# Identity products in TensorE's gaps, another order of the first loads, and a re-planned order, in a fused attention and mixture-of-attention-experts kernel

## The chip, the core and the metric

The program runs on one core of one Trainium2 chip. A core has four computing engines that run side by side, each with its own instruction stream in a fixed order: TensorE (PE, matrix products; PEld are its weight loads), VectorE (DVE), ScalarE (ACT, functions such as tanh and exp) and GpSimd (POOL). SyncE (SP) only issues transfers (DMAs) between the chip's memory and the on-chip memory; ACT and POOL can issue some too. Engines wait for each other by semaphores. The metric is the device time of one execution in microseconds (us); lower is better.

## What is computed

Two stages follow each other. The first is attention over 8 batches of 12 heads, 448 positions, head size 64, with soft-capped scores; its output, 8 x 448 x 768, is the input of the second: four causal attention experts per batch, two of them chosen for each position by a gate.

```python
def _attn_ref(q, k, v, cap):
    scores = cap * np.tanh(scale * (q @ k.T) / cap)
    attn = softmax(scores)                  # over keys
    return attn @ v

def _moe_ref(x, w_gate, wq, wk, wv, wo):
    topk = argpartition(-(x @ w_gate), 2)[..., :2]; w = softmax of the two logits
    for e in range(4):
        q, k, v = x @ wq[e], x @ wk[e], x @ wv[e]
        a = causal_softmax(q @ k.T / 8)
        out += (w of e where chosen, else 0) * (a @ v @ wo[e])
```

## The kernel before

**Tiling.** Two heads of a batch form a pair; there are 48 pairs, six to a batch. For each pair:

- loads of k, q and v into f32 staging tiles (`kst`, `vst`, four each, two pairs in one; `qf`). k and v come in three parts: 384 rows, and the last 64 rows of the even and of the odd head (`kt0`, `kt1`, `vt0`, `vt1`).
- casts to f16 (`cast`, L399): by POOL, but by DVE for some k of early pairs (`CV`) and for q and k of the first pairs; pair 0's k by ACT.
- transposes of q and k so that the head size lies on the partitions: by products with an identity on PE and a copy out of PSUM by DVE (`a_tr` L441, `a_trev` L469), and from pair 9 on for k, from pair 34 on for q too, by a transposing DMA on SP (`a_trd` L475).
- scores on PE (`sc`, L541), in three groups with one tanh each on ACT (`y`, L547): two blocks of 448 columns (tanh over 128 x 896), or three (128 x 1344). The two products of a block pair have 64 rows each and use different halves of the array.
- one exp on ACT over all seven blocks (`pbuf`, L560).
- attention times values on PE (`pv`, L572 and L577) in four parts (two PSUM tiles, two halves each), normalisation by DVE (`xk`, L589), a transpose (`xtp`, L599) and a copy to `xT`, the second stage's input.

When six pairs of a batch are done, the second stage of that batch is interleaved with the pairs that follow: values and gate (`vps`, L679), projections (`qps`, `kps`, L801), masks, scores and exp (`pS`, L827), values, output projection (`wops`, L908) and stores. Its weights `wvg`, `wq`, `wk` and `wo` are loaded by DMAs that POOL issues (L1302) between its casts.

**What sets the order.** A planner in the kernel file (class `Sched`) writes out every engine's instructions while the program is built. Each unit of work has an engine, an assumed duration, units it needs, and a due time; among the units that can start first the one with the smallest due time is taken. Transfers are given an assumed landing. Nothing is timed on the chip: an engine's instructions simply stand in the planned order and wait for their semaphores. The planner's parameters are constants at the head of the file: `EA` (earliest planned load of some pairs), `AHEAD` (how far ahead of a pair its loads are planned), `WD` (planned times of the weight DMAs), `CV`, `LATE`, and `DUES` (offsets on the due times by kind of work). The list `FIRST` fixes order and queue of the first loads by hand; SP issues most of them, ACT three:

```python
FIRST = [
    ("k", 0, 1, "SP"), ("kt0", 0, 2, "SP"), ("k", 1, 1, "SP"), ("q", 1, 1, "SP"),
    ("v", 0, 1, "SP"), ("vt0", 0, 2, "SP"), ("kt0", 2, 2, "SP"), ("kt1", 2, 2, "SP"),
    ("k", 2, 1, "SP"), ("q", 2, 1, "SP"), ("v", 1, 1, "SP"), ("k", 3, 1, "SP"),
    ("q", 3, 1, "SP"), ("vt0", 2, 2, "SP"), ("vt1", 2, 2, "SP"), ("v", 2, 2, "SP"),
    ("q", 0, 1, "ACT"), ("kt1", 0, 2, "ACT"), ("vt1", 0, 2, "ACT"),
]
```

PE begins with seven products of a zero tile (`dummy`, L1333). For pair 0, ACT casts 384 columns of k and copies their transposes, DVE does q; scores begin when both are copied.

Of the kernel before, what the change touches and what calls it, by code (L numbers as in the profile page):

```python
# [16 lines left out]
NAUX = 3  # L17
# [3 lines left out]
LATE = 7  # L21
TD = 15.0
EA = {4: 0.0, 6: 0.0, 8: 8.0, 10: 20.0, 12: 40.0, 14: 50.0}
# [3 lines left out]
CV = 8  # L27
# [3 lines left out]
AHEAD = 34.0  # L31
WD = (22.0, 26.0, 38.0, 50.0)
DUES = {
    'B0': 1, 'B2': 6, 'B3': 19, 'B4': -16, 'g5': -1001, 'gw5': 16, 'gw6': -1000, 'laff': 1,
    'lf': 8, 'lg': -1000, 'llg': -1000, 'lotev': 1000, 'lpv': 16, 'lpvev': -1000, 'lqk': 1000,
    'lv': -1, 'lwo': 1016, 'mk5': 4, 'mk6': -8, 'oa6': 1016, 'pv46': -6, 'pvB6': -4, 'pvev46':
    -2, 'pvevA': 6, 'q6': 3, 'qm6': -1000, 'v5': -2000, 'wo6': -2, 'xt45': 1, 'xtA': -5,
    'xtev45': -2, 'xtev46': 12, 'xtev47': 2, 'xtevA': 1000
# [3 lines left out]
class Sched:  # L42
# [58 lines left out]
    def arm(self, u):  # L101
# [6 lines left out]
        for d in u["deps"]:  # L108
            t, e = self.done[d]
            x = 0.0  # L110
            if e == "POOL" and u["eng"] != "POOL":
                x = max(PS, u["slack"] if u["eng"] == "PE" else 0.0)
            elif u["eng"] == "PE" and e != "PE":
                x = u["slack"]
            r = max(r, t + x)
# [3 lines left out]
    HALF = ("tr", "trq", "trk", "trt", "xt", "mk", "oT", "lot", "keep")  # L119
# [13 lines left out]
    def start(self, u, e=None):  # L133
        s = max(self.free[e or u["eng"]], u["r"])
        if u["eng"] == "DVE" and u["key"][0] in self.PORT:
            s = max(s, self.free["POOL"])
# [4 lines left out]
    def emit(self, u, e):  # L141
# [10 lines left out]
        if e == "PE":  # L152
            dur += 0.1 if self.mode == 64 else 0.0
            self.mode = 128
# [3 lines left out]
        if u["land"]:  # L158
            self.dma = max(self.dma, s + 2.0) + u["land"] / 2.15e5
            t = self.dma + 0.1 + u["lag"]  # L160
        if u["give"] is not None:
            self.bank[self.held.pop(u["give"])] = t
# [3 lines left out]
        self.finish(u["key"], t, e)  # L166

# [73 lines left out]
def kernel(  # L241
# [113 lines left out]
    def nbytes(n, which):  # L355
        t = {"q": 224 * 0.055, "k": 256 * 0.045, "v": 256 * 0.045}.get(which, 64 * 0.03)
        return n * t / 16 * 2.15e5
# [3 lines left out]
        ("k", 0, 1, "SP"), ("kt0", 0, 2, "SP"), ("k", 1, 1, "SP"), ("q", 1, 1, "SP"),  # L361
        ("v", 0, 1, "SP"), ("vt0", 0, 2, "SP"), ("kt0", 2, 2, "SP"), ("kt1", 2, 2, "SP"),
        ("k", 2, 1, "SP"), ("q", 2, 1, "SP"), ("v", 1, 1, "SP"), ("k", 3, 1, "SP"),
        ("q", 3, 1, "SP"), ("vt0", 2, 2, "SP"), ("vt1", 2, 2, "SP"), ("v", 2, 2, "SP"),
        ("q", 0, 1, "ACT"), ("kt1", 0, 2, "ACT"), ("vt1", 0, 2, "ACT"),
    ]

    def add_load(p, n, w, due, e, deps, after=0.0):
        add(
            ("ld", w, p), e, 0.62, deps, due, load_part, p, n, w,  # L370
            nc.scalar if e == "ACT" else nc.sync, land=nbytes(n, w), lag=(DF + 1.5 * (p < 4) if p < 10 else LG if p > 15 else 0.0) if p > 1 else 0.0,
# [6 lines left out]
    for x, (w, p, n, e) in enumerate(FIRST):  # L378
        d = [last.get(e)] + ([("zst", w[0], p // 2)] if len(w) > 1 else [])
        d += [("table",)] if e == "ACT" and x > 17 else []  # L380
# [20 lines left out]
    def cast(w, p, eng):  # L401
        src = staged.pop((w, p))
        cp = eng.copy if eng is nc.scalar else eng.tensor_copy
        if w == "q":
            c16["q", p] = hd.tile([QP, QC, 2, Dh], f16, name=f"q16_{p}", tag="q16", bufs=NC)
            cp(c16["q", p], src.rearrange("p h (c d) -> p c h d", c=QC))  # L406
        elif w == "k":
            c16["k", p] = hd.tile([128, KC + 1, 2, Dh], f16, name=f"k16_{p}", tag="k16", bufs=NC)
            n = KC if p == 0 else KC + 1
            cp(c16["k", p][:, 0:n], src.rearrange("p h c d -> p c h d")[:, 0:n])  # L410
            if p == 0:
                staged["kt", p] = src[:, :, KC, :]
        elif w == "kt":
            cp(c16["k", p][:, KC], src)
# [3 lines left out]
    def add_cast(p):  # L418
        for w in CASTS:
# [11 lines left out]
            if p == 0 and w == "k":  # L431
                eng, ne, c = nc.scalar, "ACT", 0.42
                add(("cast", "kt", p), "DVE", 0.2, [("cast", "k", p)] + deps[1:], due, cast, "kt",
                    p, nc.vector)
# [8 lines left out]
    def a_tr(p, what="qk"):  # L443
# [10 lines left out]
        for c in {"qk": (0, 1, 2, 3), "k": (0, 1, 2), "t": (3,)}.get(what, ()):  # L454
# [14 lines left out]
    def a_trev(p, what):  # L469
        t = qk_tile(p)  # L470
        lo, hi = {"qk": (0, S + 512), "q": (0, S), "k": (S, S + KM), "t": (S + KM, S + 512)}[what]
# [11 lines left out]
    def add_tr(p):  # L483
# [4 lines left out]
        if p == 0:  # L488
            for w, d in (("k", "k"), ("q", "q"), ("t", "kt")):
                add(("tr" + w, p), "PE", 0.14 * len(w), [("cast", d, p), ("ident",)], due, a_tr, p,  # L490
                    w, take=("tr" + w, p), slack=0.0)
                add(("trev" + w, p), "ACT" if w == "k" else "DVE", 0.4, [("tr" + w, p)], -50.0,
                    a_trev, p, w, give=("tr" + w, p))
            add(("trev", p), "-", 0.0, [("trevk", p), ("trevq", p)], -50.0, lambda: None)
            add(("tr", p), "-", 0.0, [("trt", p)], -50.0, lambda: None)
            return
        if p >= FIRST_D:
            for w in "qk" if p >= FIRST_Q else "k":
                add(("trd" + w, p), "SP", 1.2, [("cast", w, p)] + deps[2:], due - TD, a_trd, p, w,
                    land=1.05 * 2.15e5)  # L500
# [797 lines left out]
    def add_weight(key, pairs, due):  # L1298
        due += 2.0
        for i, (dst, src) in enumerate(pairs):  # L1300
            def go(dst=dst, src=src):
                nc.gpsimd.dma_start(dst, src)  # L1302
            add((*key, i), "POOL", 0.85, [], due + i, go, after=due - 2.0 + i, land=1.3 * 2.15e5)
# [26 lines left out]
    def c_dummy():  # L1330
        ps = ps_score[0].tile([128, CAPS[0], 512], f32, name="dummy", tag="sc0")
        for _ in range(7):
            nc.tensor.matmul(ps[:, 0, :], warm[:, 0:128], warm, start=True, stop=True)  # L1333

# [73 lines left out]
    add(("table",), "ACT", 1.6, [("warm",), ("ld", "kt1", 0, "issued")], -300.0, c_table)  # L1408
# [45 lines left out]

    def pairs_of(i, later=0):
# [5 lines left out]
        if i >= NK or ("trev", i) not in sch.done:  # L1461
            return None
        return i, sch.done["trev", i][0] + 0.05

    def next_fill():
# [14 lines left out]
        if ("trev", i) not in sch.done:  # L1480
            return None
        r = max(r, sch.done["trev", i][0] + 0.05)
        one = dict(r=r, dur=0.4, armed=armed, special=True, go=lambda s: go_t([i], s))
        if nf < 1 or not info[i]["rem"]:
# [39 lines left out]
    def go_x(x, s, dur):  # L1524
        b, a = x
        sc = tile_of(state["nf"] % 2)
# [12 lines left out]
    def go_t(which, s):  # L1539
        todo = []  # L1540
# [98 lines left out]
```

## Time and profile before

| what | value |
|---|---|
| median of 3 runs | 319.39 us (319.07 to 320.24) |
| the profiled execution, its own time | 319.31 us |
| its span, first to last instruction | 317.0 us |
| mean granted TensorE clock | 0.953 of full |
| ACT: tanh (L547), 144 instructions | 144.0 us |
| ACT: exp (L560), 47 instructions | 136.6 us |
| first tanh starts at | 6.58 us |
| HBM read and written over the span | 149 GB/s |

The profile was taken from one execution by the hardware profiler. "Busy" is the time in which an engine had an instruction of its own; issuing DMAs and waiting for semaphores do not count. The granted clock is the share of the full TensorE clock that the chip's throttle let through. A timeline row gives start, duration, engine and line, operation, output from input with shapes, and in brackets the idle time of the engine just before it and what ended it.

The first transfers of the trace, with issue and landing in us:

| transfer | queue | issued | landed |
|---|---|---|---|
| k of pair 0 | SP | 0.80 | 4.57 |
| q of pair 0 | ACT | 0.81 | 4.26 |
| kt0, pairs 0 and 1 | SP | 1.50 | 5.60 |
| kt1, pairs 0 and 1 | ACT | 1.51 | 5.11 |
| k of pair 1 | SP | 2.30 | 6.92 |
| vt1, pairs 0 and 1 | ACT | 2.33 | 6.19 |
| q of pair 1 | SP | 3.17 | 7.90 |
| v of pair 0 | SP | 3.75 | 8.25 |
| k, q of pair 2 | SP | 6.37, 7.00 | 9.20, 9.84 |
| v of pair 1 | SP | 7.92 | 12.17 |
| k, q of pair 3 | SP | 8.33, 8.84 | 12.73, 13.30 |

### The profile page before, as it was taken

The page shows a single profiled execution, that of the slowest core. Times are in us where ns is not written, and L with a number is a line of the kernel's source. Part 1 is how long each engine was busy: PE and PEld are TensorE (multiplying, and loading weights), DVE is VectorE, ACT ScalarE, POOL GpSimd, SP SyncE. Part 2 cuts the span into 40 slices and gives each one's busy share as a digit, 9 for nine tenths or more (in the row PEclk, how much of TensorE's full clock was granted, in tenths as well). Part 3 has the DMA queues.
Part 4 walks back from the last instruction along what each step waited for, and adds up shares of the span by engine and source line. Part 5 has one row for each costly group of instructions (what it writes and reads, how often), then busy time and mean ns, then how long its engine had stood idle before and what let it go on. Part 6 is the DMA issues. An engine that isn't in the chain of part 4 may idle for free.

```text
span 317.0 us, 8054 instructions
## 1 busy us (share of the span) xinstructions
PE 273.1 (86%) x3073; PEld 175.3 (55%) x3073; DVE 203.2 (64%) x660; ACT 290.1 (92%) x229; POOL 177.3 (56%) x342
## 2 busy tenths in 40 slices
PE   6678669988899989998899989998899989989891
PEld 2355435665556655566656655765456755656650
DVE  2177442757667586667876675688577677664972
ACT  4889997999999999999999999999999999995631
POOL 6579690599707774498512993994419834421500
PEclk9577987999999999999999999999999999999978
DMA  6999999475979349961899484955988751020027
GB/s 158 270 280 216 232 200 185 109 152 127 276 189 223 81 113 216 302 151 36 232 260 226 82 205 83 290 174 118 278 250 198 165 104 63 0 77 2 0 97 254
DMA packets 93190, 52.87 MB, mean 167 GB/s; under 512 B 53792, under 2 KB 89760, under 8 KB 93152
## 3 DMA queue, kind: packets, MB, share of 16 engines
q1 hardware_dynamic: 81888, 50.19, 64.9%
q0 software_dynamic: 10512, 1.58, 7.0%
q10 hardware_dynamic: 752, 0.59, 0.8%
q8 instruction: 24, 0.39, 0.5%
q14 instruction: 14, 0.11, 0.2%
HBM read 36.19 MB, written 11.01 MB: 149 GB/s over the span
## 4 chain that ended last, share of the span: by engine, by line
ACT 60%; PE 24%; issue 5%; DVE 5%; POOL 2%; DMA 1%; POOLq 0%; ACTq 0%; DVEq 0%
ACT pbuf L560 28%; ACT y L547 26%; PE sc L541 5%; ACT pS L827 4%; PE pv L577 3%; PE sc L820 2%; PE vps L679 2%; PE qps L801 2%; PE pv L572 2%; DMA kst<-in_k_dram 1%; PE kps L801 1%; PE end L1050 1%; POOL ee L741 1%; PE wops L908 1%; PE xtp L599 1%
## 5 line engine op out<-in xcount | busy, mean ns | idle before, releaser
L547 ACT ACTIVATE y<-sc 128x896 f16<-128x896 f32 x144 | 144.0, 1122 | 5.2 <-PE sc L541 5.2
L560 ACT ACTIVATE pbuf<-y 128x3136 f16<-128x3136 f16 x47 | 136.6, 2906 | 0.0
L541 PE MATMUL sc<-qk 64*128 64x448 f16 (+1 forms) x336 | 63.1, 371 | 10.9 <-ACT y L547 6.8
L577 PE MATMUL pv<-v,pbuf 128*128 128x65 f16 x1140 | 60.7, 196 | 0.0
L577 PEld LDWEIGHTS <-pbuf 128*128 128x128 f16 x1152 | 53.5, 99 | 5.3 <-issue 2.5
L572 PE MATMUL pv<-v,pbuf 128*128 128x130 f16 x190 | 43.1, 227 | 13.0 <-ACT pbuf L560 10.1
L541 PEld LDWEIGHTS <-qk 64*128 64x128 f16 (+1 forms) x336 | 20.1, 94 | 44.3 <-issue 37.3
L406 POOL CAST q<-qf 112x512 f16<-112x512 f32 x46 | 28.2, 615 | 26.0 <-DMA qf<-in_q_dram 25.7
L589 DVE TENSOR_TENSOR xk<-pv,rc 128x256 f16<-128x256 f32 x95 | 40.3, 424 | 3.3
L727 POOL COPY mb<-mk 128x1024 f16<-128x1024 f16 x14 | 14.2, 1039 | 48.5 <-DVE mk L722 48.5
L572 PEld LDWEIGHTS <-pbuf 128*128 128x128 f16 x192 | 18.9, 98 | 25.6 <-ACT pbuf L560 15.4
L588 DVE RECIPROCAL rc<-pv 128x4 f32<-128x4 f32 x95 | 16.8, 177 | 23.5 <-PE pv L577 23.0
L416 POOL CAST v<-vst 128x512 f16<-128x512 f32 x48 | 28.3, 616 | 6.4 <-DMA vst<-in_v_dram 6.2
L835 POOL TENSOR_TENSOR pS<-pS,keep 128x128 f16<-128x128 f16 (+1 forms) x56 | 21.0, 395 | 15.9 <-ACT pS L827 14.3
L629 DVE COPY xT<-xtp 128x448 f16<-128x448 f16 x48 | 18.4, 386 | 17.4 <-PE xtp L599 17.4
L923 DVE COPY ob<-wops 128x384 f32<-128x384 f32 (+1 forms) x48 | 25.5, 554 | 5.9 <-PE wops L908 5.2
L679 PE MATMUL vps<-wvg,xT 128*128 128x260 f16 x168 | 29.0, 283 | 0.0
L410 POOL CAST k<-kst 128x512 f16<-128x512 f32 x42 | 25.7, 614 | 0.5 <-DMA kst<-in_k_dram 0.3
L908 PE MATMUL wops<-wo,oT 128*128 128x384 f16 x112 | 24.9, 326 | 0.5 <-DVE o L873 0.2
L741 POOL TENSOR_TENSOR ee<-euler,lg 128x16 f32<-128x16 f32 x7 | 20.4, 2913 | 8.6 <-DVE lg L686 8.6
L801 PE MATMUL qps<-xT,wq 128*128 128x448 f16 x84 | 23.3, 366 | 0.0
L801 PE MATMUL kps<-xT,wk 128*128 128x448 f16 x84 | 22.2, 352 | 0.9 <-DVE ob L923 0.4
(172 smaller groups left out, 429.6 us busy)
## 6 DMA issues: line engine op xcount, KB each, us to landing
qf<-in_q_dram SPq DMA_DIRECT2D x22, 448.0 KB, 5.5
vst<-in_v_dram SPq DMA_DIRECT2D x23, 384.0 KB, 5.0
kst<-in_k_dram SPq DMA_DIRECT2D x22, 384.0 KB, 4.7
out_dram<-ob SPq DMA_DIRECT2D x18, 384.0 KB, 3.0
kst<-in_k_dram SPq DMA_DIRECT2D x47, 32.0 KB, 4.9
vst<-in_v_dram SPq DMA_DIRECT2D x47, 32.0 KB, 4.4
out_dram<-ob SPq DMA_DIRECT2D x6, 192.0 KB, 2.9
out_dram<-vst SPq DMA_DIRECT2D x3, 384.0 KB, 2.3
```

The lines of the kernel that those rows point to most:

```text
L406: cp(c16["q", p], src.rearrange("p h (c d) -> p c h d", c=QC))
L410: cp(c16["k", p][:, 0:n], src.rearrange("p h c d -> p c h d")[:, 0:n])
L416: cp(v16[p % NV][:, :, :, 0:Dh], src)
L541: nc.tensor.matmul(o, kk[r, 128 * c : 128 * (c + 1)], qs, start=True, stop=True)
L547: nc.scalar.activation(ytile[i][:, first : first + nb, :], sc[:, 0:nb, 0:S], AF.Tanh, scale=isc / capf)
L560: nc.scalar.activation(ptile[i], ytile.pop(i), AF.Exp, scale=capf)
L572: nc.tensor.matmul(pv[:, n, :, :], ptile[i][:, idx[0, KC], w : w + 128], v16[i % NV][:, :, KC, :], start=(n == 0), stop=False, skip_group_ ...
L577: nc.tensor.matmul(pv[:, n, g, :], ptile[i][:, idx[g, c], w : w + 128], v16[i % NV][:, g, c, :], start=False, stop=(c == KC - 1), skip_gro ...
L589: nc.vector.tensor_tensor(xk, pv[:, :, :, 0:Dh], rc.broadcast_to((128, 2, 2, Dh)), ALU.mult)
L679: nc.tensor.matmul(ps, xT[b][:, j, w : w + 128], wvg[:, j, :], start=(j == 0), stop=(j == NDC - 1),)
L801: nc.tensor.matmul(s[which, r], w2[r][:, j, :], xT[b][:, j, :], start=(j == 0), stop=(j == NDC - 1),)
L908: nc.tensor.matmul(ps, s["oT"][:, r, w : w + 128], wo2[r][:, f * (D // 2) : (f + 1) * (D // 2)], start=(r == 0), stop=(r == 1),)
```

## The change

Four things change.

1. Products of the identity with itself, 128 columns each, are put where the planner sees PE idle before 60 us of planned time (`keep_warm`, `warmer`). Their output is never read. The program has 76 of them, in groups.
2. The first loads change order and queue: q of pair 1 goes to ACT's queue, `vt1` to SP's. Pair 0's k is cast and transposed in three pieces (128 columns by ACT, 256 by DVE, the tail by DVE), and scores may begin when the first piece is there. Pair 1's q and k are transposed and copied separately.
3. The planner's model of transfers (bytes by kind, latency, lag) and of some port rules has other numbers.
4. `DUES`, `EA`, `AHEAD`, `WD`, `CV` and `LATE` have other values, so that the planned order differs over most of the program.

```diff
-LATE = 7
+LATE = 9
-EA = {4: 0.0, 6: 0.0, 8: 8.0, 10: 20.0, 12: 40.0, 14: 50.0}
+EA = {4: 0.0, 6: 0.0, 8: 20.0, 10: 12.0, 12: 52.0, 14: 30.0}
-CV = 8
+CV = 6
-AHEAD = 34.0
-WD = (22.0, 26.0, 38.0, 50.0)
+WARM = 60.0
+AHEAD = 37.0
+WD = (18.0, 26.0, 40.0, 50.0)
 DUES = {
...
@@ def emit(self, u, e):
         if e == "PE":
+            self.keep_warm(s)
...
-            self.dma = max(self.dma, s + 2.0) + u["land"] / 2.15e5
+            self.dma = max(self.dma, s + (2.6 if s < 3.0 else 2.2)) + u["land"] / 2.15e5
...
+    def keep_warm(self, s):
+        f = self.free["PE"]
+        n = int((s - f - 0.1) / 0.115)
+        if not 4.0 < f < WARM or s > 1.0e6 or n < 3:
+            return
+        i = min(range(NAUX), key=lambda i: self.bank[i])
+        if self.bank[i] > f:
+            return
+        self.nw = getattr(self, "nw", 0) + n
+        self.warm(self.pool.tile([128, 512], f32, name=f"warm_{self.nw}", tag=f"aux{i}"), n)
...
-        ("k", 0, 1, "SP"), ("kt0", 0, 2, "SP"), ("k", 1, 1, "SP"), ("q", 1, 1, "SP"),
-        ("v", 0, 1, "SP"), ("vt0", 0, 2, "SP"), ("kt0", 2, 2, "SP"), ("kt1", 2, 2, "SP"),
+        ("k", 0, 1, "SP"), ("kt0", 0, 2, "SP"), ("k", 1, 1, "SP"), ("v", 0, 1, "SP"),
+        ("vt0", 0, 2, "SP"), ("vt1", 0, 2, "SP"), ("kt0", 2, 2, "SP"), ("kt1", 2, 2, "SP"),
...
-        ("q", 0, 1, "ACT"), ("kt1", 0, 2, "ACT"), ("vt1", 0, 2, "ACT"),
+        ("q", 0, 1, "ACT"), ("kt1", 0, 2, "ACT"), ("q", 1, 1, "ACT"),
...
+            lo, hi = {"k": (0, 1), "kb": (1, KC), "kt": (KC, KC + 1)}[w] if p == 0 else (0, KC + 1)
+            cp(c16["k", p][:, lo:hi], src.rearrange("p h c d -> p c h d")[:, lo:hi])
...
-                eng, ne, c = nc.scalar, "ACT", 0.42
-                add(("cast", "kt", p), "DVE", 0.2, [("cast", "k", p)] + deps[1:], due, cast, "kt",
-                    p, nc.vector)
+                eng, ne, c = nc.scalar, "ACT", 0.25
+                add(("cast", "kt", p), "DVE", 0.2, deps[1:], due, cast, "kt", p, nc.vector)
+                add(("cast", "kb", p), "DVE", 0.33, deps[0:1], due, cast, "kb", p, nc.vector)
...
+    def warmer(ps, n):
+        for _ in range(n):
+            nc.tensor.matmul(ps[:, 0:128], ident, ident, start=True, stop=True)
+
+    sch.warm = warmer
```

PE's order at the first pairs, as the two programs have it (number of products; `tr` are transposes of a pair, `sc` score groups, three to a pair, `pv a` and `pv b` the two tiles of attention times values):

```
before: dummy 7 | q0 4, k0 3, tail 1 | sc0 2, sc1 2, sc2 3 | tr1 8 | sc3 2, sc4+sc5 5
        | pv0 a, pv0 b | tr2 8 | pv0 a, pv0 b | sc6 2, sc7 2 | tr3 8 | sc8 3 ...
after:  dummy 7 | q0 4, k0 1, k0 2 | sc0 2, sc1 2 | tail 1 | 3 products | q1 4 | sc2 3 | k1 4
        | 5 products | sc3 2 | 9 products | sc4+sc5 5 | tr2 8 | 9 products | tr3 8
        | pv0 a, pv0 b, pv0 a, pv0 b | sc6 2 | x0 4 | sc7 2, sc8 3 ...
```

Further on, groups of 8, 16, 13 and 13 products stand before the pv of pairs 1, 3, 4 and 5. On DVE, the cast of q1 stands before the copy of pair 0's tail transpose. On POOL, the casts come in the order v0, k2, q2, v1, k3, q3 (before: v0, v1, k2, q2, k3, q3), and the four DMAs of `wk` stand after the casts of k10, k11, v9 and v10 (before: ahead of all four but v9). On SP, the loads of pairs 14 and 15 stand before the transposing DMAs of pairs 9 to 11, and the loads of pairs 12 and 13 after the transposing DMAs of pairs 14 and 15. ACT's sequence is unchanged but for the two first copies and the place of two exps of the second stage (`pS` of batch 0). On every engine the last instructions, the second stage of the last two batches and the last pairs' scores, stand as before.

## The prediction

> **What bounds the kernel now.** I read the page first: which engine is nearly always busy, and in which of the 40 slices something is off.
>
> ```profile
> PE 273.1 (86%) x3073; PEld 175.3 (55%) x3073; DVE 203.2 (64%) x660; ACT 290.1 (92%) x229; POOL 177.3 (56%) x342
> PEclk9577987999999999999999999999999999999978
> ```
>
> ScalarE (ACT) works 290.1 of 317.0 us; 26.9 us are idle. The clock row shows TensorE throttled in the first seven slices, some 55 us. The table of stretches then says where ACT idles: 8.7 us before 60, none from 60 to 280 (a row of it below), 18.1 after 280.
>
> ```profile
> 80.00:120.00 40.00, 35.96 (x432) 23.60 (x430) 27.50 (x90) 40.00 (x31) 22.86 (x41) 1.00 0.70 174
> ```
>
> The order of the last pair and the last batch is the same in both programs, so the 18.1 us at the end stay. ACT's operations are the same too, but for two copies cut from 384 to 128 columns. The change can therefore earn only what ACT waits before 60 us, and lose by new waits after it. ACT's waits, then its timeline at those waits (start, duration, in brackets the idle time before it):
>
> ```profile
> ACT y L547 <- PE sc L541: 5.2, 6, 1.8
> ...
> 8.63 1.29 ACT L547 ACTIVATE y<-sc 128x1344 f16<-128x1344 f32 x1 [0.32 <-PE sc L541]
> 10.74 0.92 ACT L547 ACTIVATE y<-sc 128x896 f16<-128x896 f32 x1 [0.82 <-PE sc L541]
> 17.75 0.92 ACT L547 ACTIVATE y<-sc 128x896 f16<-128x896 f32 x1 [1.40 <-PE sc L541]
> 29.14 0.92 ACT L547 ACTIVATE y<-sc 128x896 f16<-128x896 f32 x1 [0.29 <-PE sc L541]
> 53.03 0.92 ACT L547 ACTIVATE y<-sc 128x896 f16<-128x896 f32 x1 [1.79 <-PE sc L541]
> ```
>
> All five are tanh waiting for scores: 4.6 us, and 0.56 before the first tanh at 6.58. So 5.2 us is the whole stake of the first 60.
>
> **The clock.** It changes at multiples of 3.41 us from 3.94. I cut the span there (PE busy, PEld, DVE, ACT, POOL, granted clock, DMA, GB/s):
>
> ```profile
> 3.94:7.36 3.42, 1.74 (x14) 0.69 (x13) 1.46 (x5) 1.77 (x3) 1.91 (x20) 1.00 0.83 217
> 17.60:21.01 3.41, 1.86 (x19) 0.93 (x15) 2.89 (x21) 3.26 (x2) 2.12 (x4) 1.00 1.12 294
> 31.25:34.66 3.41, 2.01 (x43) 1.59 (x40) 1.75 (x6) 3.41 (x4) 2.82 (x6) 1.00 1.66 226
> 41.49:44.90 3.41, 1.36 (x24) 0.89 (x24) 0.13 (x1) 3.41 (x3) 3.41 (x8) 1.00 1.26 252
> 44.90:48.32 3.42, 2.97 (x21) 1.32 (x20) 1.47 (x5) 3.42 (x3) 1.97 (x4) 0.50 1.66 206
> ```
>
> After the first, second and fourth the clock is 0.50 in the next window; after the third it stays at 1.00. Busy time (1.86 against 2.01) hardly separates them; streamed columns do. Summed over the matmuls of each window (the two 64-row products of a score pair run side by side and count once) they are 0.23, 0.29 and 0.25 of what full clock could stream where the clock fell (8192 columns), and 0.38 (34.66:38.07) and 0.44 where it stayed. So the bound lies between 0.29 and 0.38, 2400 to 3100 columns a window.
>
> The Trainium skill, "TensorE: Matmul & The Clock Gate", section "Why this matters for your kernels", allows PE-idle gaps up to some 3 us. By it the products would be useless, since PE's longest idle stretch in the cooled window 41.49 to 44.90 is 2.05 us; the row shows a fall all the same. By the rule the sum below would lose its 1.79; the measurement decides.
>
> **Part 1, the products (L1366).** 76 in the program, 128 columns each, all before the first batch's projections: groups of 3, 5, 9, 9, 8, 16, 13, 13. A transpose of that size steps at 0.11 us at half clock (0.63 for four at 8.76) and about 0.055 at full (0.39 for four at 18.01, 0.22 of it the first one's latency).
> - 41.49 window: 13 products are 1664 columns, 0.25 + 0.20 = 0.45: above the bound. Then the block of scores, values and q projections in front of the sc at 52.57 runs at full clock: 5.9 us (46.64 to 52.57) become about 3.5 (5.09 of them halve), and the stall of **1.79** goes, with 0.6 to spare. If only half of the 13 fall into the window, 0.35 is between the bounds and the stall may stay.
> - 17.60 window: 8 products add 1024 columns, 0.29 + 0.12 = 0.41. The pair's four pv parts at 24 to 28 us then take 0.25 instead of 0.41 each, and **0.29** at 29.14 goes.
> - First window: only 3 products fall in it; 0.23 + 0.05 + the 448 columns of pair 1's q if they come in time = 0.28 to 0.33. I take it that the clock falls at 7.36 as before.
> They hide in PE's waits, except where they run at half clock right before ready work: nine cost 0.96 us (counted below).
>
> **Part 2, loads, casts and transposes of pairs 0 to 3.**
> - First tanh. ACT's cast of k falls from 0.51 to about 0.30 us (384 to 128 columns; 0.83 ns a column from the 0.92 and 1.29 of tanh), its copy from 0.48 to 0.27. Then the q copy on DVE, which ends at 5.18 + 0.39 = 5.57 now, decides; scores follow 0.16 later as now, tanh 0.40 after them: 6.13 instead of 6.58.
> - Pair 1. q1 moves from third on SP to ACT's queue, issued at 2.33 instead of 3.17, beside k1 on SP. Now q1 lands 4.7 us after issue (7.90), k1 4.6 (6.92). No row has two large first loads side by side: q1 lands at 6.6 at best (224 KB behind kt1's 5.11, at 150 of the first window's 217 GB/s) and 7.9 at worst (as now). I take 7.2. New waits: DVE's cast of q1 stands ahead of the tail copy that sc needs, and on PE the transposes of q1 stand ahead of pair 0's third scores; both now wait for that landing. From it, at half clock: cast 0.43, transposes 0.37, three scores 0.75, four k transposes 0.43 and latency 0.20, copy 0.41, gaps 0.14, scores 0.59 = 3.3. Pair 1's tanh starts at 10.5 (9.9 to 11.2) instead of 10.74; third scores come at 9.1, a wait of about 1.1, inside this number.
> - The skill's "DMA: Bandwidth & Descriptors", section "Queues, rings and completion order", says that each DMA engine takes turns between the queues with work; by that both k1 and q1 would end near 7.4, my estimate, and the tanh at 10.7. No run here shows it.
> - Pair 2, the 1.40. Now POOL casts v1 first, which lands late, and k2, q2, k3, q3 queue behind it:
>
> ```profile
> 12.22 0.62 POOL L416 CAST v<-vst 128x512 f16<-128x512 f32 x1 [3.04 <-DMA vst<-in_v_dram]
> ...
> 14.45 0.61 POOL L406 CAST q<-qf 112x512 f16<-112x512 f32 x1
> ```
>
>  After the change k2 and q2 (landed 9.84) go ahead of v1, so pair 2's transposes leave PE's way. But pair 3's now stand before pv of pair 0: q3 lands 13.30 as now (the same bytes are ahead of it), its cast is third behind v1 and k3 and ends at 13.33 + 0.61 = 13.94. PE at half clock: nine products, 1.04 of scores, 0.9 of pair 2, nine products end about 14.36. That fills the window to 14.18 (0.48), so the clock rises there as it did after 0.48 at 17.60. Then 0.45 (pair 3) + 4 x 0.25 (pv) + 0.08 + 0.40 (scores) = 16.3. ACT itself would be ready at 10.5 + 5.61 = 16.1 (14.37 and 16.35 less 10.74 now). So tanh of pair 2 starts at 16.3 instead of 17.75: **1.45**, which holds the gains and losses of all steps before it. Ends: 15.95 without the products' wait, 17.3 if the clock stays at half (0.92 + 1.65 + 0.6).
>
> **Part 3, the rest of the order.** From pair 4 on loads, casts and POOL's weight DMAs move. Cover: ACT is never idle after 60 in the present kernel. Two places lose cover, since ACT will be 3.5 us earlier:
> - POOL issues wk behind v10 (lands 42.14): 42.8 to 45.3 instead of 39.2 to 41.7. PE meets the second head pair's k projection ahead of sc of pair 9, at about 55 (57.33 now, less 3.5, and 1.2 of work), and can wait until 57.3 before ACT does (its tanh at 62.16 now, less 3.5 and 1.3 for the scores and projections between).
>
> ```profile
> DMA to landing us min/median/max: 8.3/9.4/13.6
> ```
>
>  The last of the four then lands 45.3 + 8.3 to 13.6 = 53.6 to 58.9: no stall by three of the four, 1.6 by the longest (the last one now). I take a quarter, **0.4**.
> - Pairs 14/15 load before 12/13. Pair 12's loads wait on SP behind the transposes of 14 and 15, so its k transpose, landed at 66.24 now, comes 3 to 6 us later, for scores due at about 72.8 (tanh at 76.89 now, less 3.5 and 0.6). No loss, little left.
> CV = 6 moves two casts (0.43 each) from DVE to POOL (0.61): nothing, DVE is 64% busy.
>
> **Sum.** Profiled execution 319.31 (span 317.0 + 2.3; the median of the runs is 319.39). 319.31 - 1.45 - 0.29 - 1.79 + 0.4 = **316.2**.
>
> **Rivals.**
> 1. *Forecast*, 0.52: 315.0 to 317.6.
> 2. *The clock falls anyway*, 0.18. For: 0.41 and 0.45 are near the bound, and the windows need not fall on the same work. Against: the longest idle stretch is filled. 1.79 and 0.29 stay, pair 2 gains 0.35 to 1.45: 317.9 to 319.0.
> 3. *Nothing gained at pair 2*, 0.14: q1 late in ACT's queue, or pair 3's transposes hold pv. Only 2.08 gained: 317.6 with the 0.4.
> 4. *A late transfer takes back more than was won*, 0.16, the slower side. Place: pair 12's k on SP. Now one k transpose took 3.9 us of its own on the busy queue (landings 50.65 and 54.54); the loads of 12 stand behind four of those instead of two, and their casts behind them on POOL. A stall begins when the transpose lands after 72.8, 6.6 us later than now; it decides from 3.5 more, 76.3. Two more transposes at 3.9 are 7.8, and 384 and 448 KB of pair 16 ahead at about 2 us each make 12: lands 78.2, a stall of 5.4, time 321.6. Against: most land in 3.1 us (median).
>
> **How the numbers follow.** 0.5% is 1.6 us, about what this kernel's runs can tell from no change: faster means under 317.8. Case 1 and four fifths of 3 are there (0.63); 2 mostly within (0.20 with strays of 3 and 4); 4 mostly slower (0.17). The range leaves out two in ten: from 314.9 (pair 2 at 15.95 and no wk stall give 315.3, with a little for the rest of the 5.2) to 320.5, inside case 4. The likeliest's own is 315.0 to 317.6.
>
> **What would show it.** Clock: 1.00 from about 14 us, no fall at 21.0 and 44.9; a 0.50 there with a stall near 50 is case 2. Tanh starts: 6.1, 10.5, 16.3; the last decides case 3. ACT idle from 20 to 280: none but at most 1.6 at 58; an idle time at 72 released by a DMA is case 4. The end, from the last exp on, as now; a different one would prove me wrong at once.

## The result and the profile after

The changed kernel takes 318.74 us (median of 22 executions, 317.21 to 321.95), the kernel before 319.23 (22 executions, 317.57 to 324.21). The ratio is 0.9989, with a 95% interval from 0.9965 to 1.0013: no change that can be measured. (An execution more than 1.5% above the fastest of its kernel counts as slow: ratios, here and below, leave such executions out, medians do not.) The forecast was 316.2, a gain of 3.1 us. The profiled execution of the changed kernel took 318.50 us, its span is 316.7 (before 319.31 and 317.0).

The page of the changed kernel shows nearly the same work on ACT (289.7 us, 290.1 before), and a clock that is full almost from the start, with one dip in the fifth slice, one in the tenth and three at the end (two before):

```profile
PE 273.8 (86%) x3149; PEld 177.6 (56%) x3149; DVE 203.9 (64%) x661; ACT 289.7 (91%) x229; POOL 178.6 (56%) x344
PEclk9999799997999999999999999999999999999887
```

So in the first 60 us the clock did what the change is for, and more than was forecast. Next, ACT's waits (total, times, longest) and its timeline at the waits for scores, in the changed kernel:

```profile
ACT y L576 <- PE sc L570: 3.7, 4, 2.0
...
6.28 1.73 ACT L576 ACTIVATE y<-sc 128x896 f16<-128x896 f32 x2 [0.48 <-PE sc L570]
8.95 2.10 ACT L576 ACTIVATE y<-sc 128x1344 f16<-128x1344 f32 x2 [0.94 <-PE sc L570]
16.02 0.92 ACT L576 ACTIVATE y<-sc 128x896 f16<-128x896 f32 x1 [0.28 <-PE sc L570]
40.13 0.92 ACT L576 ACTIVATE y<-sc 128x896 f16<-128x896 f32 x1 [2.01 <-PE sc L570]
```

The row at 16.02 is the tanh of pair 2, at 17.75 before: 1.73 us won. The waits that stood at 29.14 and 53.03 are gone. But a wait of 2.01 us stands before 40.13, where the kernel before had none. Ahead of it, PE and POOL stand like this (timeline of the changed kernel):

```profile
33.21 0.93 PE L570 MATMUL sc<-qk 64*128 64x448 f16 x5
35.47 1.17 POOL L422 CAST q<-qf 112x512 f16<-112x512 f32 x2 [2.76 <-DMA qf<-in_q_dram]
36.13 0.45 PE L465 MATMUL trq<-ident,q 112*128 112x112 f16 x4 [1.99 <-POOL q L422]
36.38 1.59 PE L1366 MATMUL warm<-ident 128*128 128x128 f16 x13
37.76 0.32 PE L601 MATMUL pv<-v,pbuf 128*128 128x130 f16 x1
39.66 0.37 PE L570 MATMUL sc<-qk 64*128 64x448 f16 x2
```

PE works in its written order, and next in it is the transpose of pair 9's q. Pairs 8 and 9 share one load of q, and that lands at 35.34 (29.97 before), so PE stands from about 34 to 36.13. The 13 products that were planned into a gap run after it, ahead of pair 4's pv, which had been due since pair 4's exp ended at 36.13. Of the 1.63 us by which that pv is late, the transpose takes the first 0.45 and the products most of the rest. And the 3.41-us window in which PE stood has few columns, 0.25 of the 8192 that full clock could stream, and the next one runs at half clock (rows of the table of stretches: busy time of PE, PEld, DVE, ACT and POOL, granted clock, DMA share, GB/s):

```profile
32.88:36.30 3.42, 1.31 (x11) 0.58 (x12) 0.92 (x3) 3.42 (x3) 0.83 (x2) 1.00 1.72 199
36.30:39.71 3.41, 3.41 (x47) 3.31 (x44) 0.74 (x3) 1.82 (x2) 2.07 (x4) 0.50 1.41 261
```

The scores come at 39.66, and ACT (1.82 us busy in the second row) has waited 2.01.

### The profile page after: what moved, and what is told of

Read it like the earlier page. It is cut to its first block, busy times and chain, and to the rows that moved or that the text cites. A ratio compares the mean times of both kernels' runs of the same rounds, so it can differ in the third digit from the quotient of the medians.

```text
span 316.7 us, 8214 instructions
## 1 busy us (share of the span) xinstructions
PE 273.8 (86%) x3149; PEld 177.6 (56%) x3149; DVE 203.9 (64%) x661; ACT 289.7 (91%) x229; POOL 178.6 (56%) x344
## 3 DMA queue, kind: packets, MB, share of 16 engines
q0 software_dynamic: 10512, 1.58, 9.9%
## 4 chain that ended last, share of the span: by engine, by line
ACT 62%; PE 14%; DMA 10%; issue 5%; POOL 4%; DVE 2%; SPq 1%; ACTq 0%; POOLq 0%; DVEq 0%
ACT pbuf L589 28%; ACT y L576 28%; DMA qf<-in_q_dram 6%; ACT pS L856 4%; PE sc L849 2%; DMA kst<-in_k_dram 2%; PE sc L570 2%; PE pv L606 2%; DMA vst<-in_v_dram 1%; PE end L1079 1%; PE vps L708 1%; POOL ee L770 1%; PE pv L601 1%; DMA out_dram<-vst 1%; POOL mb L756 1%
## 5 line engine op out<-in xcount | busy, mean ns | idle before, releaser
L570 PE MATMUL sc<-qk 64*128 64x448 f16 (+1 forms) x336 | 61.3, 359 | 8.4 <-ACT y L576 5.6
L606 PE MATMUL pv<-v,pbuf 128*128 128x65 f16 x1140 | 58.9, 194 | 0.0
L606 PEld LDWEIGHTS <-pbuf 128*128 128x128 f16 x1152 | 52.3, 98 | 3.7 <-issue 1.1
L601 PE MATMUL pv<-v,pbuf 128*128 128x130 f16 x190 | 42.7, 225 | 10.8 <-ACT pbuf L589 7.7
L431 POOL CAST v<-vst 128x512 f16<-128x512 f32 x48 | 28.7, 619 | 10.9 <-DMA vst<-in_v_dram 5.3
L601 PEld LDWEIGHTS <-pbuf 128*128 128x128 f16 x192 | 18.8, 98 | 23.7 <-ACT pbuf L589 13.6
L429 POOL CAST k<-kst 128x512 f16<-128x512 f32 x44 | 26.9, 614 | 2.6 <-DMA kst<-in_k_dram 1.4
L708 PE MATMUL vps<-wvg,xT 128*128 128x260 f16 x168 | 27.9, 275 | 0.0
L830 PE MATMUL qps<-xT,wq 128*128 128x448 f16 x84 | 22.5, 352 | 0.0
L830 PE MATMUL kps<-xT,wk 128*128 128x448 f16 x84 | 21.5, 353 | 0.0
```

The costliest lines, as they stand in the source:

```text
L429: cp(c16["k", p][:, lo:hi], src.rearrange("p h c d -> p c h d")[:, lo:hi])
L431: cp(v16[p % NV][:, :, :, 0:Dh], src)
L570: nc.tensor.matmul(o, kk[r, 128 * c : 128 * (c + 1)], qs, start=True, stop=True)
L601: nc.tensor.matmul(pv[:, n, :, :], ptile[i][:, idx[0, KC], w : w + 128], v16[i % NV][:, :, KC, :], start=(n == 0), stop=False, skip_group_ ...
L606: nc.tensor.matmul(pv[:, n, g, :], ptile[i][:, idx[g, c], w : w + 128], v16[i % NV][:, g, c, :], start=False, stop=(c == KC - 1), skip_gro ...
L708: nc.tensor.matmul(ps, xT[b][:, j, w : w + 128], wvg[:, j, :], start=(j == 0), stop=(j == NDC - 1),)
```

## The experiments

All times are medians of the whole execution. "Pair 1" and "pair 12" are the starts of those pairs' exp in the run's one trace, "idle" is ACT's idle time from 20 to 65 us (gaps over 0.2 us), "tail" runs from the start of the last exp to the end of the span. "k10" is the load of pair 10's k. Each ratio is to the kernel before in the same session. Its medians there were 319.23 (the four runs of the first round), 319.07 (third round), 319.24 and 318.45 (fourth round; the last for "before + products, tail too, the same again" and for the last row), so across sessions the ratios are to be compared, not the medians.

| kernel | n | median us | ratio to before, 95% | pair 1 | idle | pair 12 | tail |
|---|---|---|---|---|---|---|---|
| before, three traces | | | | 18.56, 18.90, 18.20 | 2.08, 0.56, 0.24 | 83.15, 82.34, 81.19 | 29.28, 29.77, 29.24 |
| after, three traces | 22 | 318.74 | 0.9965 to 1.0013 | 16.83, 16.43, 16.94 | 2.01, 3.04, 1.80 | 81.51, 82.06, 81.55 | 30.69, 30.92, 31.83 |
| after, no products | 12 | 318.41 | 0.9950 to 1.0012 | 18.36 | 0.00 | 81.02 | 29.98 |
| after, without the 13 | 12 | 318.77 | 0.9942 to 1.0009 | 17.22 | 3.16 | 83.19 | 29.87 |
| after, k10 behind pair 8 | 12 | 318.99 | 0.9969 to 1.0031 | 17.01 | 6.97 | 86.96 | 29.48 |
| after, weights late again | 12 | 318.19 | 0.9934 to 1.0008 | 17.96 | 2.95 | 83.85 | 29.75 |
| after, both of these | 12 | 318.91 | 0.9951 to 1.0015 | 17.08 | 0.80 | 80.51 | 29.91 |
| the same, weights at 26 | 12 | 318.45 | 0.9962 to 1.0020 | 17.91 | 1.82 | 83.35 | 29.38 |
| before, weights at 18 | 12 | 318.49 | 0.9968 to 1.0020 | 18.78 | 0.59 | 82.22 | 29.30 |
| after, no weight traffic | 9 | 316.81 | 0.9891 to 0.9949 | 16.81 | 0.00 | 79.22 | 30.07 |
| before + products | 12 | 317.98 | 0.9937 to 1.0004 | 16.83 | 4.86 | 84.34 | 29.92 |
| the same again | 12 | 318.35 | 0.9935 to 0.9998 | 17.10 | 2.35 | 81.97 | 29.73 |
| before + products, tail too | 6 | 316.35 | 0.9873 to 0.9944 | 18.23 | 0.63 | 81.55 | 28.35 |
| the same again | 12 | 317.51 | 0.9924 to 0.9981 | 17.83 | 2.08 | 82.61 | 28.34 |
| after + tail products | 12 | 317.71 | 0.9922 to 0.9979 | 17.04 | 3.11 | 82.96 | 28.81 |
| after, loads as before, tail products | 12 | 316.71 | 0.9902 to 0.9961 | 16.70 | 1.13 | 80.60 | 29.06 |

**First round: the products and pair 10's k.** No products at all:

```diff
-WARM = 60.0
+WARM = 0.0
```

> The changed kernel without any of its 76 products (the order of all else is unchanged). Theory: in the changed kernel the second transposed q (pair 9's) stands on PE ahead of pair 4's pv, and 13 products stand between them; PE gets to them at 36.38, when pair 4's pv is already due (its exp ended at 36.13), and at half clock they hold it until 37.66. Without them that pv starts some 1.3 us earlier and the 1.95-us idle of ACT at 38.12 falls to 0.6 to 0.9. Against it stands that the window that read .34 of wide columns (without the products of 18.16) reads .26 and the clock falls near 19, which cost before 0.29. So about 318.7 - 1.0 = 317.7 (317.2 to 318.2). Rival, the prediction's: the products are what removes the stalls at 29.14 and 53.03 (0.29 and 1.79), and without them it is 318.7 + 1 to 2 = 319.7 to 320.8.

Measured: 318.41, and no idle time at all from 20 to 65 us. The time lies 0.2 us over the theory's range; the rival's 319.7 falls. But the trace says something else as well: PE ran at half clock until 27.13 (four transposes take 0.55 to 0.58 us up to there, 0.36 at full clock; the first clock record of this trace is the rise at 27.13, so its clock row shows nothing of it). Pair 2's wait is back (ACT's timeline without products):

```profile
17.55 0.92 ACT L576 ACTIVATE y<-sc 128x896 f16<-128x896 f32 x1 [1.20 <-PE sc L570]
18.36 2.81 ACT L589 ACTIVATE pbuf<-y 128x3136 f16<-128x3136 f16 x1
```

The new order of the first loads and casts, alone, brings pair 1's exp to 18.36, against 18.20 to 18.90 before. It is the clock that moves it to 16.8. What the clock wins there is gone by pair 12: ACT, 1.5 us later here at pair 1, meets its loads in time and starts pair 12's exp at 81.02, against 81.51 in the changed kernel.

Without the group of 13 only, and with pair 10's k behind pair 8's loads:

```diff
-        if not 4.0 < f < WARM or s > 1.0e6 or n < 3:
+        if not 4.0 < f < WARM or 30.0 < f < 39.0 or s > 1.0e6 or n < 3:
```

> The changed kernel without the one group of 13 products that stands between pair 9's transposed q and pair 4's pv; the other 63 stay. Theory: the group costs 1.3 us at that place (it runs late, at half clock), so ACT's idle at 38.12 falls from 1.95 to about 0.6 and the time to 318.7 - 1.3 = 317.4. Rival: pair 8's q, which lands at 35.34, is the whole cost and PE would be late with or without the group: idle at 38.12 stays 1.7 to 2.0, time 318.5 to 318.9.

```diff
-EA = {4: 0.0, 6: 0.0, 8: 20.0, 10: 12.0, 12: 52.0, 14: 30.0}
+EA = {4: 0.0, 6: 0.0, 8: 8.0, 10: 20.0, 12: 52.0, 14: 30.0}
```

> The changed kernel with the load of pair 10's k issued behind pair 8's loads again, as before (two numbers of one table; loads, casts and products of the pairs around it follow, the rest of the order is unchanged). Theory: pair 8's q lands near 30 in place of 35.34, pair 9's transposed q no longer waits on PE, the window of 32.88 keeps its clock, ACT's idle at 38.12 (1.95) goes, and nothing else is late: 318.7 - 1.95 = 316.8. Rival: the loads share one bandwidth, so pair 10's k or q is late in its turn and the same stall stands one pair later: 318.3 to 318.9.

Measured: 318.77 and 318.99. Both theories (317.4 and 316.8) fall as to the time. The 13 products alone are not the cost: without them no wait stands at 38, though pair 8's q lands at 36.04, but waits stand at 27.5, 42.7 and 46.0 instead, and at the second of them PE stands 3.11 us for pair 10's q. With k10 moved, pair 8's q still landed at 36.68; the one trace is that kernel's longest execution (322.84), so its five waits, at 32.8 to 61.2, prove nothing. This second edit is also less clean than the first: the planner works its order out anew, and pair 9's transpose stands elsewhere on PE.

The kernel before with the function `keep_warm` and its three calls, nothing else (74 products; the order of all else on PE stays):

> The kernel before with the products put into its own planned gaps (74 of them, nothing else changed). Theory, as the prediction had it: the half-clock stretches from 21.01 and 44.90 go, and with them the stalls at 29.14 (0.29) and 53.03 (1.79): 319.3 - 2.1 = 317.2, with ACT's idle at 51.24 (1.73) gone. Rival: the stall of 53.03 was the order of the loads and transposes ahead of pair 8, not the clock: 318.9 to 319.4 and the idle stays.

Measured: 317.98. Its one trace was the slowest of its executions but shows pair 1's exp at 16.83, the very time of the changed kernel, with the old order of loads. The wait at 53 is gone, waits at 27, 37 and 41 stand in its place.

**Second round: what repeats.** Two more traces of each of the two kernels.

> The changed kernel unaltered, a second look. Theory: the stalls between 20 and 65 us belong to the execution, not to the program: where the loads of that execution land (pair 4's k landed between 17.5 and 18.5 in four programs that issue it alike, its v between 21.2 and 24.6) and where the edges of the clock's 3.41-us windows lie against it. So pair 1's exp starts at 16.8 to 17.3 again, but the idle of ACT from 20 to 65 us is somewhere between 0 and 6 us and at other places than 38.12, and pair 12's exp starts within 81 to 85 instead of at 81.51. Rival: the stall of 1.95 at 38.12 is the program's (pair 10's k ahead of pair 8's loads, 13 products behind a late transpose): it comes again at 37.8 to 38.5 with 1.7 to 2.2, and pair 12's exp starts at 81.2 to 81.8.

> The same, a third look: theory, pair 12's exp anywhere from 81 to 85, idle of ACT from 20 to 65 us different from both earlier looks by over 0.5; rival, 81.2 to 81.8 and the stall of 38.12 again.

> The kernel before unaltered, a second look. Theory: pair 1's exp at 18.2 to 18.8 again (that stall is the program's: PE at half clock from 7.36), but the stall of 1.79 at 53.03 does not come at that place; idle of ACT from 20 to 65 us between 0 and 6, pair 12's exp between 82 and 86. Rival: the stalls of 29.14 (0.29) and 53.03 (1.79) come again within 0.3 of size and place, pair 12's exp at 82.9 to 83.4.

> The same, a third look: theory, pair 12's exp anywhere from 82 to 86 and the idle differently placed; rival, 82.9 to 83.4 and the stall of 53.03 again.

The answer is mixed, and it is the key to the case. In the changed kernel the wait at 38 comes again (ACT's timeline, second and then third trace):

```profile
40.78 0.92 ACT L576 ACTIVATE y<-sc 128x896 f16<-128x896 f32 x1 [3.04 <-PE sc L570]
```

```profile
39.81 0.92 ACT L576 ACTIVATE y<-sc 128x896 f16<-128x896 f32 x1 [1.56 <-PE sc L570]
```

It belongs to the program; its size, 1.56 to 3.04, belongs to the execution. (With tail products, below, the head is the same, and the wait there is 1.06.) In the kernel before the wait at pair 2 repeats (1.40, 1.40, 1.39), but the 1.79 at 53.03 does not. Second trace, then third:

```profile
52.02 0.92 ACT L547 ACTIVATE y<-sc 128x896 f16<-128x896 f32 x1 [0.56 <-PE sc L541]
```

```profile
17.39 0.92 ACT L547 ACTIVATE y<-sc 128x896 f16<-128x896 f32 x1 [1.39 <-PE sc L541]
...
49.07 2.90 ACT L547 ACTIVATE y<-sc 128x1344 f16<-128x1344 f32 x3
```

In the last row three tanh follow one another without a wait, at the place where the first trace lost 1.79.

**Third round: which loads.** The weights' start times, alone, with k10 (the edit of `EA` above), later still, and in the kernel before:

```diff
-WD = (18.0, 26.0, 40.0, 50.0)
+WD = (22.0, 26.0, 38.0, 50.0)
```

> The changed kernel with the start times of the expert weights' loads put back to those of before (22, 26, 38, 50 in place of 18, 26, 40, 50); pair 10's k stays ahead of pair 8's loads. Theory W (the weights take the transfer time that pair 8's loads need: in the changed kernel the first weight is issued at 17.7 in place of 21.2 to 24.4, and pair 8's q lands at 35.1 to 36.0 in place of 30.0 to 31.8): pair 8's q lands 2 to 4 us earlier, at 31.5 to 33.5, and the stall at 38 (2.0, 3.0 and 1.6 us in three looks) falls under 0.8; time about 317.5. Theory K (pair 10's k, issued ahead of pair 8's, is what delays them): q lands at 34.5 to 36 still, the stall is 1.5 to 3, time 318.5 to 319.

> As the run before, and pair 10's k behind pair 8's loads as well. Theory W: pair 8's q lands 0 to 2 us earlier than in the run before, no stall over 0.8 near 38, time 317 to 317.5. Theory K: now q lands at 30 to 32.5 and the stall goes, time about 316.8, while the run with the weights alone kept it. Both fall if a stall of over 1.5 us stands anywhere between 20 and 65 us: then it is the sum of the loads that lags, in whatever order, and the gain at pair 2 is only waited for later (318.5 to 319).

> As the run before, with the weights four more us later (26, 30, 40, 50). Theory W: pair 8's q lands as early as in the kernel before or earlier (29 to 31), the ACT engine has under 0.8 of idle time from 20 to 50 us; a stall is left only if the weights are now late for the first products with them near 47 (then 1 to 2 us there): 316.5 to 317.5 without it. Theory K: as in the run before. Theory of the sum of the loads: the idle time merely moves to 47 and after, 318.5 to 319.

> The kernel before with the expert weights' first loads at 18 in place of 22 (one number; nothing else of the change). Theory W: pair 8's q, which landed at 30.0, 31.8 and 31.2 in three looks, lands 2 to 4 us later, at 33 to 35, and an idle of ACT of 0.5 to 2 appears between 33 and 45 us; time 319.2 + 0 to 1. Theory K: pair 8's q moves by under 1 us and no idle appears there; time 318.9 to 319.4.

Pair 8's q landed at 34.70, 30.48, 31.70 and 32.34. Since the loads before it are early in one execution and late in another, the fair measure is the time from the landing of pair 6's q to that of pair 8's. It is 5.0 to 7.1 us in nine traces with both as before, 7.7 with k10 ahead alone, 9.2 with the weights early alone (both in the kernel before and in the changed one, there in its longest execution), and 9.4 to 10.9 with both. So the weights do most of it (theory W), k10 adds some 1 to 2; neither theory alone holds, since 34.70 is what K said and 36.68 in the first round what W would have said. The landings can be compared in this way, the waits less so: these four programs are planned anew too. With the weights late again the 13 products ahead of pair 4's pv are gone (64 products in place of 76) and a pair's transposes stand behind a score group in place of ahead of it. With both put back the wait at 38 shrinks to 0.59 (by the loads or by this order, which is open) and pair 12's exp starts at 80.51, the earliest of the kernels that compute everything; yet that kernel's twelve executions have a median of 318.91 (315.74 to 321.06). With the weights at 26 ACT idles 0.52 and 1.30 us before 45 and 52 instead; at the second of them PE stands for a DVE copy that waits for POOL, not for a weight, and POOL had stood for pair 12's q, which landed at 49.36. That is what the third theory in these expectations says, that the sum of the loads lags: the wait moves to a later load. The run without the 13 products fits it as well. With the weights early in the kernel before, an idle time of 0.59 appears at 40.21, as W said, but no loss (318.49). By time, none of the four can be told from the others, nor from the two kernels.

**Fourth round: the traffic, and the tail.** Nine weight loads replaced by setting their tiles to zero on GpSimd, at the same places in the same order:

```diff
-                nc.gpsimd.dma_start(dst, src)
+                if key[1] in ("wvg", "q"):
+                    nc.gpsimd.memset(dst, 0.0)
+                else:
+                    nc.gpsimd.dma_start(dst, src)
```

> The changed kernel without the nine loads of the gate, value and query weights of the experts (issued from 17.7 to 30 us): GpSimd sets their tiles to zero at the same places, the order of all else is unchanged. The second stage's output is left out by it. Theory (between 15 and 45 us the sixteen DMA queues are the limit, so ACT cannot run ahead of the pairs' loads, and what was gained at pair 2 is waited for later): pair 8's q lands 3 to 6 us before the 35.1 to 36.0 of the three looks, the stall at 38 goes, pair 12's exp starts at 79.0 to 80 instead of 81.5 to 82.1, and the time falls by about 2 to 316.8. Rival (PE's order, that is the late transpose and the 13 products behind it, and the clock make the stall): it stays over 1 us, pair 12's exp at 81 to 82, time 318.3 to 319.

Measured: 316.81, ratio 0.9920 (0.9891 to 0.9949), clear of the changed kernel's; pair 12's exp at 79.22, no idle time from 20 to 65. The rival falls: transpose and products stand in the same order, and PE comes through them well ahead of pair 4's pv, which now waits for ACT (PE's timeline without weight traffic):

```profile
34.22 0.37 PE L465 MATMUL trq<-ident,q 112*128 112x112 f16 x4
34.43 0.89 PE L1369 MATMUL warm<-ident 128*128 128x128 f16 x13
36.17 0.23 PE L601 MATMUL pv<-v,pbuf 128*128 128x130 f16 x1 [0.85 <-ACT pbuf L589]
```

Pair 8's q came only 1.7 to 2.6 us earlier (33.43) and not 3 to 6; that was enough. From issue to landing it took 6.45 us here, 9.6 to 10.8 in the three traces of the changed kernel and 6.0 to 7.9 in those of the kernel before. While it was under way the DMA engines moved about as many bytes but were far less busy (rows of the table of stretches, first of the changed kernel, then without weight traffic; the last two numbers are DMA share and GB/s):

```profile
25.00:30.00 5.00, 4.31 (x63) 3.06 (x63) 2.04 (x6) 5.00 (x5) 4.59 (x7) 1.00 1.69 240
30.00:35.00 5.00, 3.25 (x47) 2.08 (x47) 2.08 (x6) 5.00 (x5) 2.71 (x5) 1.00 1.40 221
```

```profile
25.00:30.00 5.00, 3.56 (x55) 2.53 (x56) 2.07 (x6) 5.00 (x5) 2.89 (x6) 1.00 0.83 242
30.00:35.00 5.00, 4.66 (x74) 3.33 (x72) 2.38 (x7) 5.00 (x5) 3.96 (x9) 1.00 1.09 234
```

The kernel before was not run without these loads. Since ACT idles 0.96 us from 20 to 65 there on the mean, and not at all between 60 and 280 in its first trace, it could hardly gain more than that; this is argued, not shown.

The repeat of the products alone, and products in the tail:

> The kernel before with products in its own gaps, again, since its twelve executions had a mean span of 315.65 against 316.93 of the kernel before (69 executions) but its one profile was among the slowest. Theory (the products are the part of the change that pays, and the rest of it gives nothing): ratio 0.996 to 0.998, 0.6 to 1.3 us faster. Rival (chance draw of twelve): within 0.3 us of the kernel before.

```diff
-        if not 4.0 < f < WARM or s > 1.0e6 or n < 3:
+        if not (4.0 < f < WARM or f > 280.0) or s > 1.0e6 or n < 3:
             return
+        if f > 280.0:
+            n = max(n, 9)
```

> The kernel before with products as in the last, and 27 more after 280 us: nine ahead of the last transposed batch's products (where PE stands about 1 us for GpSimd), nine ahead of the output products of the tail, nine near 284. Theory (in ten looks the window that begins some 10 us after the last exp read .27 to .31 and the clock fell for 3.4 or 6.8 us near 13 us after it; where it did not fall, the tail's copies came 0.9 to 2.0 us earlier): no half clock between the last exp and 24 us after it, the tail 0.9 to 1.5 us shorter, time 0.9 to 1.5 below the run without them, about 317.0. Rival (the output's stores set the end): the copies come earlier and the span ends within 0.3.

> The changed kernel with 18 products in the tail, at the same two places. Theory: as there, 318.8 - 0.9 to 1.8 = 317.0 to 317.9 and a tail of 29 to 30 us in place of 30.7 to 31.8. Rival: within 0.3 of the changed kernel.

> The fastest so far again (the kernel before with products in its own gaps of the first 60 us and of the tail), which had only six executions to compare: 316.0 to 317.2, ratio 0.990 to 0.994, and a tail of 28.3 to 28.9 us with no half clock between the last exp and 24 us after it. Rival: a draw; 317.5 to 318.3 as without the tail's products.

> The changed kernel with the weights' start times and pair 10's k as before and 18 products in the tail. If the head in its new order is worth something beside products and loads, this is the fastest, 315.8 to 316.3; if the head is worth nothing, it equals the kernel before with the same products, 316.2 to 317; if the new order of the loads costs nothing on the mean, it equals the changed kernel with tail products, 317.3 to 318.1.

The products alone make the kernel before faster, 0.9967 (0.9935 to 0.9998) in the repeat, if barely beyond the interval. With the tail's products the ratio goes from 0.9989 to 0.9951 on the changed kernel (some 1.2 us) and from 0.9967 to 0.9908 and 0.9953 on the kernel before with products (some 1.9 and 0.5 us). The intervals overlap in each case, so on times alone this is not shown; the traces say more. The stretches of the tail (PE, PEld, DVE, ACT, POOL, clock, DMA share, GB/s) show why, first in the changed kernel and then with products in its tail:

```profile
296.00:300.00 4.00, 2.61 (x35) 1.86 (x32) 3.65 (x17) 1.94 (x2) 2.79 (x6) 0.89 0.00 0
300.00:304.00 4.00, 3.43 (x36) 2.00 (x35) 2.21 (x10) 1.46 (x4) 0.00 (x0) 0.68 0.00 0
```

```profile
296.00:300.00 4.00, 3.96 (x61) 3.07 (x58) 3.69 (x14) 2.84 (x3) 3.56 (x9) 1.00 0.00 0
300.00:304.00 4.00, 2.71 (x41) 1.80 (x39) 3.05 (x16) 1.40 (x3) 0.59 (x1) 1.00 0.00 0
```

The clock stays at 1.00. ACT's first copy of the last batch's output comes 17.0 us after the last exp in each trace with tail products, and 17.9 to 19.0 in the traces of both kernels without. It also comes at 17.0 in the two traces without tail products in which the clock happened not to fall there (k10 behind pair 8, weights at 26): so it is the clock, not the products as such.

A version that beats both kernels is the changed one with its loads put back and products in the tail: ratio to the kernel before 0.9931 (0.9902 to 0.9961), that of the changed kernel 0.9989 (0.9965 to 1.0013). The kernel before with products in both places reached 0.9908 and 0.9953 in its two series; which of the two versions is better stays open.

## Why the prediction was wrong

- **The step that failed** is Part 3, "Two places lose cover, since ACT will be 3.5 us earlier". There is a third, and it decides. The two named ones cost nothing: the last wk landed at 52.59, and no wait follows pair 12's k, so the 0.4 was not there either. What was counted at nothing is the first weight at 17.66 in place of 21.18 and k of pair 10 ahead of pair 8's loads. With them pair 8's q lands 4.5 us later on the mean of the traces (35.5 in place of 31.0), with PE's transpose of pair 9's q, and 13 products behind it, ahead of pair 4's pv. "ACT is never idle after 60" is no cover for a load that is needed at 36. Of the traces' means: pair 1's exp is 1.8 us earlier (18.55 to 16.73), ACT then idles 2.28 from 20 to 65 in place of 0.96, and at pair 12 0.5 us are left (82.23 to 81.71). The forecast had that idle time 2.08 smaller; it came out 1.32 larger. The run without the weights' traffic gives 1.9 us back; that is shown. That the two loads, put back, would do so on the mean is not: the one trace says yes, twelve executions do not.
- **The term 1.79** was mis-sized. It was the right price of that one execution, and an accident of it: 1.79, 0.56 and nothing in three traces. The 0.29 at 29.14 is small in all (0.29 in the first, none in the second, 0.24 in the third).
- **The clock's bound** nearly held. It was put between 0.29 and 0.38 of 8192 columns. In 20 traces (1677 windows at full clock) no window under 0.36 kept the clock, and 56 of the 59 falls came at 0.38 or less; the other three came at 0.40, 0.41 and 0.44, so between 0.36 and 0.44 both happen. The 17.60 and 41.49 windows of the kernel before had 0.29 and 0.25.
- **"I take it that the clock falls at 7.36 as before"** was wrong in the good direction: the window 5.58 to 8.99 held 0.41 and the clock stayed. It was near: 0.44 in the first window of the changed kernel with tail products did not keep it. In the second trace the clock rose only at 9.38, and pair 1's exp came at 16.43 even so. What gives pair 2 its gain is full clock from some 9 us on; the kernel before with products, in the old order, has it and comes to 16.83 and 17.10. The order of the head seems to count where the clock is still or again half after 8 us and full from 12 us at the latest: six traces of the new order lie at 16.4 to 17.2 then, two of the old at 17.8 and 18.2. That is a pattern of single traces, not a test.
- **Pair 2's tanh** was forecast at 16.3 and came at 16.02. The steps to it were close (first tanh 6.28 for 6.13, q1's landing 7.44 for 7.2), but the agreement is in part luck: 16.3 was worked out for half clock until 14.18, and in the two traces that had this about (until 13.39 and 14.77) the tanh came at 17.1. By the Trainium skill's "DMA: Bandwidth & Descriptors", section "Queues, rings and completion order", k1 and q1 would both end near 7.4, by the prediction's estimate; they landed at 7.68 and 7.44, which agrees.
- **The rivals.** 318.74 lies in the range of rival 2 (317.9 to 319.0), but not for its reason: 1.79 and 0.29 did not stay, and the clock fell at 36.30, behind a late load. In kind it is rival 4, a late transfer that takes back what was won, at pair 9's q in place of pair 12's k, and smaller.
- **"The end, from the last exp on, as now"** was wrong too. The three traces have a mean tail of 31.1 us against 29.4. Some 0.4 of it lies behind the last landing: from there to the end of the span it is 1.6 us in the changed kernel (1.4 to 1.6 in its variants) against 1.2, which is nearly made up outside the span: from span to whole time it is 2.3 us before and 1.9 after on the mean. Much of the rest is the clock, which fell for 6.8 us near 13 us after the last exp in two of the three traces (3.4 in the third, and in those of the kernel before); the tail products show its price. That the changed kernel draws the longer fall more often is not shown.

## What to carry to other kernels

A stall in one profile is a draw: take two or three traces before you add up stalls, and count only what comes back. When ACT is made earlier, price first the loads that it will then meet; here 1.3 of the 1.8 us won at pair 2 were waited for again, most of it at pair 6. Products that fill a known wait pay where nothing is late behind them, as in the tail. Where the wait is for a load they run behind it and hold up what is due next, as ahead of pair 4's pv; that this costs time on the whole is not shown (318.77 without that group, 318.74 with it).

## What the hardware showed that was not expected

- The edges of the clock's windows lie differently in every execution: the first change of clock came at 3.94, 5.27 and 5.65 us in three traces of the kernel before, and later changes follow in steps of 3.41 us. So the same program loses clock at other places, and other waits stand.
- The transfers that GpSimd issues cost far more of the DMA engines per byte than those of SP. In the queue table of the changed kernel (packets, MB, share of 16 engines; the first row is SP's queue, the second GpSimd's):

```profile
q1 hardware_dynamic: 81792, 49.99, 64.4%
q0 software_dynamic: 10512, 1.58, 9.9%
```

 Per MB this is 1.3% of the span on the first and 6.3% on the second. Per packet they are close, 40 and 48 ns: SP's packets have 611 bytes on the mean, the weights' 150. From 18 to 42 us of this trace the 128-byte packets of the weights took 32 ns, SP's of 256 bytes 23 and of 768 bytes 49. So most of the difference is short packets; whether the issuing engine adds to it is open. The 1.58 MB take 31 us of all sixteen engines (9.9% of 316.7; 7.0% in the kernel before).
- The same load lands up to 5 us apart from one execution to the next: v of pair 4, issued at 13.8 to 14.7 in the three traces of the kernel before and in the first of the same kernel with products, landed at 19.53, 22.65, 21.99 and 24.57.
